# A scheduled attention and feed-forward kernel: Strassen's form in the output product too, a and b in one PSUM bank, and the first batch given to the scheduler

## The chip, the cores and the metric

The kernel runs on one core of one Trainium2 chip. The metric is the device time of one execution in microseconds (us), as the median of several executions. Each profile is of one execution. A profile's span is some 1.9 us shorter than the time.

Engines in the profile: PE is TensorE's matmuls, PEld its weight loads (they overlap PE), DVE is VectorE, ACT is ScalarE, POOL is GpSimd, SP is SyncE.

## The reference

```python
# q, k, v: (8 batches, 8 heads, 576, 64) f32; out: (4608, 512) f32
kv  = einsum('bhsd,bhse->bhde', k, v)
x   = einsum('bhsd,bhde->bhse', q, kv)
x   = x / sqrt(mean(x*x, -1) + 1e-6) * g_norm        # per head; then (4608, 512)
a, b = x @ w_a, x @ w_b                              # (512, 1536) each
out = (a * b) @ w_out                                # (1536, 512)
```

## The kernel before

The program is straight-line code that a small list scheduler inside the kernel writes. Each piece of work is a node with an engine, a planned duration, a priority, the nodes it needs and the buffers it takes and frees. The scheduler plays these nodes through with the planned durations and emits them in the order it finds. Nothing in the program changes that order at run time: each engine is given its own queue of instructions.

```python
class Plan:
    LAT = {"PE": 0.27, "SP": 2.2}            # from a node's end to whoever waits for it; others 0.1
    def ready(self, n):
        t = 0.0
        for d, lat in n.deps:
            if d.end is None: return INF
            t = max(t, self.after(d, 0.0 if lat is None and d.eng == n.eng else lat))
        for b in n.takes:
            t = max(t, b.ring.when(), b.ring.pool.pick()[0])
        return t
def mm_us(n, cols):  return n * (cols / 2400 + 0.0025)
def act_us(n, bias=False): return (0.26 if bias else 0.16) + n / 1200
def dve_us(n):       return (n + 151) / 960          # fp32, or from PSUM
def fast_us(n):      return (n / 2 + 100) / 960      # 16-bit, SBUF only
```

The first 512 tokens go through the plain a/b products. The other 4096 go in blocks of 512 to 768 tokens through Strassen's seven products in Winograd's form, with operand sums made on VectorE. For each of six column blocks j, and for a and b apart, the seven products come in the order below. X, Y and Z are PSUM banks, `ev` is a copy out of a bank on ScalarE, `comb` an addition of a bank and such a copy on VectorE. A product onto a bank that is being read must wait for the read.

```python
PB, PA = Pool(banks[0:5]), Pool(banks[5:8])
RX, RY, RO = (Ring(PB, c) for c in (2, 2, 1))        # a/b: X; Y and Z; output product
RQ, RS = Ring(PA, 2), Ring(PA, 2)                    # attention
# [...] in wino_block, for which in ("a", "b"), for each j (arguments shortened):
p1 = pe(X, b11);  e1 = ev(u1, X)
p2 = pe(Y, b21);  c11 = comb(Y, u1)                  # frees Y
p6 = pe(X, t2);   e2 = ev(u2, X)                     # onto X: waits for e1
p5 = pe(Z, t1);   p7 = pe(X, t3);  e3 = ev(u3, X)
c22 = comb(Z, u3)
p4 = pe(X, t4);   c21 = copy(X)                      # ScalarE; frees X
p3 = pe(Z, b22);  c12 = comb(Z, u2)                  # onto Z: waits for c22; frees Z
# [...]
m = mul(ab, a_part * b_part)                         # VectorE, when a and b are there
```

The output product is the plain one: for each of 36 groups of 128 tokens, twelve matmuls of 512 columns in nodes of three, and one copy by VectorE or ScalarE. The k of a late batch (2 to 7) is put in another order by VectorE, `"p h c d -> p c h d"`, with 4 chunks of 128 rows and one of 64 apart. Batch 0 is written by hand ahead of everything that is scheduled.

Of the kernel before, what the change touches and what calls it, by code (L numbers as in the profile page):

```python
# [40 lines left out]
class Buf:  # L41
# [6 lines left out]
    def take(self, t=0.0):  # L48
        r = self.ring
        i = r.pool.pick()[1]  # L50

        self.tile = r.pool.tiles[i]
        r.pool.holder[i] = self
        r.held = [b for b in r.held if b.freed() > t] + [self]
        return self


class Node:
    def __init__(self, eng, dur, prio, emit, deps=(), takes=(), frees=()):
        self.eng, self.dur, self.prio, self.emit = eng, dur, prio, emit  # L60
        self.deps = [d if isinstance(d, tuple) else (d, None) for d in deps if d is not None]
        self.takes = takes
        self.start = self.end = None
        for b in frees:
            b.last.append(self)


class Plan:
    LAT = {"PE": 0.27, "SP": 2.2}
# [28 lines left out]
    def order(self):  # L98
        free, todo, done = {}, sorted(self.nodes, key=lambda n: n.prio), []
        waits = {n: [d for d, _ in n.deps if d.end is None] for n in todo}  # L100
        while todo:
            best = {}
            for n in todo:
                if waits[n]:
                    waits[n] = [d for d in waits[n] if d.end is None]
                    if waits[n]:
                        continue
                f = free.get(n.eng, self.t0)
                if n.eng in best and best[n.eng][0][0] <= f:
                    continue  # L110
                t = max(self.ready(n), f)
                if t == INF:
                    continue
                key = (f if t < f + 0.06 else t, n.prio)
                if n.eng not in best or key < best[n.eng][0]:
                    best[n.eng] = (key, t, n)
            assert best, "no node can go"
            _, t, n = min(best.values(), key=lambda x: x[1])
# [10 lines left out]
def kernel(  # L129
# [27 lines left out]
    WB = [0, 128] + list(range(256, d_ff + 1, 256))  # L157
# [3 lines left out]
    BLOCKS = [(512, 320), (1152, 256), (1664, 320), (2304, 384), (3072, 384), (3840, 384)]  # L161
    NMAX = 384
    NJ = FC // 2

# [5 lines left out]
    def sb(name, shape, dt):  # L170
# [7 lines left out]
    sums = {w: [sb(f"s{w}{i}", [128, 2, HM], FP16) for i in range(4)] for w in "ab"}  # L178
    xp = [sb(f"xp{i}", [128, 2, R], FP16) for i in range(2)]
    k_ts = [sb(f"k_t{i}", [128, H * EC * D], BF16) for i in range(2)]  # L180
    v_ts = [sb(f"v_t{i}", [128, H * EC * D], BF16) for i in range(2)]
# [3 lines left out]
    T_ts = [sb(f"T{i}", [128, 4, 2, NMAX], FP16) for i in range(2)]  # L185
    b_ts = [sb(f"b_sb{i}", [128, 2, 2 * NMAX], FP16) for i in range(2)]
    u_ts = [sb(f"u{i}", [128, NMAX], FP32) for i in range(8)]
    sq_ts = [sb(f"sq{i}", [128, HF], BF16) for i in range(4)]
    rs_ts = [sb(f"rs{i}", [128, HF], FP32) for i in range(4)]
    o_ts = [sb(f"o_sb{i}", [128, d_model], FP32) for i in range(4)]  # L190

    arenas = [
        [ab_ts[1][:].rearrange("p a b -> p (a b)"), 0],
        [T_ts[0][:].rearrange("p a b c -> p (a b c)"), 0],
        [T_ts[1][:].rearrange("p a b c -> p (a b c)"), 0],
        [b_ts[1][:].rearrange("p a b -> p (a b)"), 0],
    ]

    def carve(n, dt=BF16):
        w = n * (2 if dt == FP32 else 1)  # L200
        for a in arenas:
            if a[1] + w <= a[0].shape[1]:
                ap = a[0][:, a[1] : a[1] + w].bitcast(dt)
                a[1] += w
                return ap
        raise ValueError(n)
# [4 lines left out]
    def early_load(t, b, hs):  # L211
        for n, src in (("q", q), ("k", k), ("v", v)):
# [6 lines left out]
        {  # L219
            "q": early_view(carve(H * EC * D)),  # L220
            "k": early_view(k_ts[b]),
            "v": early_view(v_ts[b]),
        }
        for b in range(2)
# [4 lines left out]
    for n, src, eng in (("q", q, nc.scalar), ("k", k, nc.sync), ("v", v, nc.sync)):  # L229
        raw[n] = carve(2 * EC * D, FP32)[0:EP].rearrange("p (h c d) -> p h c d", h=2, d=D)  # L230
# [6 lines left out]
    qs = [[carve(S) for _ in range(NP)] for _ in range(2)]  # L237


    zt = const.tile([128, 512], BF16)  # L240
# [10 lines left out]
    for i in range(2):  # L251
        t = const.tile([128, NP, 128], BF16, name=f"kvd{i}")
        nc.vector.memset(t, 0.0)
        kvd.append(t)
    g_col = const.tile([128, 1], FP32)
# [9 lines left out]
    for f0, f1 in zip(WB[:-1], WB[1:]):  # L265
# [3 lines left out]

    for i in range(2):  # L270
        early_load(early[1], 1, slice(i * HP, (i + 1) * HP))
# [5 lines left out]
    early_ring = {"at": [banks[0:3], 0], "f": [banks[4:8], 0]}  # L277

    def bank(kind):
        r = early_ring[kind]  # L280
        r[1] += 1
        return r[0][(r[1] - 1) % len(r[0])]

    def dummies(n):
        ps = banks[3]
# [6 lines left out]
    class Attn:  # L292
        def __init__(self, b):
            self.b, self.kvd = b, kvd[b % 2]
# [67 lines left out]
    at0 = Attn(0)  # L362
    n_sq, n_rs = [0], [0]

    def nxt(ts, n):
        n[0] += 1
        return ts[(n[0] - 1) % len(ts)]

    def qT0(p):
        ps = bank("f")  # L370
        at0.early_qT_mm(p, ps)
        at0.early_qT_out(p, ps, nc.vector.tensor_copy)

    def kv0(p, cp):
        ps = bank("f")
        at0.early_kv_mm(p, ps)
        at0.early_kv_out(p, ps, cp)

    def xu0(p, h):
        at0.x_mm(p, h, bank("at"))  # L380
        at0.sq_op(p, h, nxt(sq_ts, n_sq))

    def norm0(p, h):
        at0.rs_op(p, h, nxt(rs_ts, n_rs))
        at0.xt_op(p, h)

    def ss0(p, h, norm=True):
        at0.s_mm(p, h, bank("f"))
        if norm:
            norm0(p, h)  # L390

# [8 lines left out]

    N0 = BLOCKS[0][0]

# [12 lines left out]
    qT0(0)  # L415
    kv0(0, nc.vector.tensor_copy)
    dummies(3)
    xu0(0, 0)
    xu0(0, 1)
    last = NP - 1  # L420
    for p in range(1, NP):
        qT0(p)
        dummies(6 if p == 1 else 4)
        kv0(p, nc.scalar.copy if p == last else nc.vector.tensor_copy)
        ss0(p - 1, 0)
        if p == last:
            dummies(2)
        xu0(p, 0)
        ss0(p - 1, 1, norm=p != last)
        xu0(p, 1)  # L430
    dummies(1)
    ss0(last, 0)
    norm0(last - 1, 1)
    ss0(last, 1)
    lead = [[bank("f"), bank("at")], [bank("f"), bank("f")]]

    def lead_mm(u, *kcs):
        for kc in kcs:
            for ps, w in zip(lead[u], (wa_t, wb_t)):
                std_mm(ps, w, u, kc, N0)  # L440

    lead_mm(0, 0, 1, 2)
    lead_mm(1, 0, 1, 2)
    lead_mm(0, 3)
    std_a(lead[0][0], 0)
    std_b(lead[0][1], 0)
    lead_mm(1, 3)
    std_a(lead[1][0], 1)
    std_b(lead[1][1], 1)

# [4 lines left out]
    def act_us(n, bias=False):  # L455
        return (0.26 if bias else 0.16) + n / 1200

    def dve_us(n):
        return (n + 151) / 960

    def fast_us(n):
        return (n / 2 + 100) / 960

    T0 = 24.5
    plan = Plan(T0)
    PB, PA = Pool(banks[0:5]), Pool(banks[5:8])
    RX, RY, RO = (Ring(PB, c) for c in (2, 2, 1))
    RQ, RS = Ring(PA, 2), Ring(PA, 2)
    RU, RB, RT, RAB = Ring(u_ts), Ring(b_ts), Ring(T_ts), Ring(ab_ts)
    RSQ, RRS, ROS = Ring(sq_ts), Ring(rs_ts), Ring(o_ts)  # L470
    RK, RV, RKR, RQT, RKD = Ring(k_ts), Ring(v_ts), Ring([kr_t]), Ring(qT_ts), Ring(kvd[::-1])
    normed = {}

    def xdeps(pairs, ta, tb):
        return [
            normed[b, p, h]
            for b in range(1, B)
# [6 lines left out]
    readers = {}  # L484

# [33 lines left out]
    def early_batch(b, win):  # L519
# [5 lines left out]
        for p in range(NP):  # L525
            pr = w0 + (w1 - w0) * (p - 0.7) / NP
            sq, sk = Buf(RY), Buf(RY)
            here = [plan.at(37.0 if p < NP // 2 else 40.5)]
            n1 = plan.add("PE", 0.40, pr, lambda p=p, s=sq: at.early_qT_mm(p, s.tile), here, [sq])
# [5 lines left out]
            n3 = plan.add("PE", 0.35, pr, lambda p=p, s=sk: at.early_kv_mm(p, s.tile), here, [sk])  # L535
# [7 lines left out]
    def late_batch(b, load, win):  # L543
# [3 lines left out]
        kr = Buf(RKR)  # L547
        kd = Buf(RKD)
# [5 lines left out]
        def reorder():  # L554
            src = view(kb.tile)
            nc.vector.tensor_copy(
                kr.tile[:, 0:NCH], src[:, :, 0:NCH, :].rearrange("p h c d -> p c h d")
            )
            nc.vector.tensor_copy(kr.tile[0:SB, NCH], src[0:SB, :, NCH, :])

        r = plan.add("DVE", 1.2, w0, reorder, [(load["n"], 7.0)], [kr], [kb])
        s = Buf(RS)

        def kv_mm():
            kv_ps = s.tile[:].rearrange("p (a e) -> p a e", a=NP)
            for c in range(NCH + 1):
                rows = 128 if c < NCH else SB
                for p in range(NP):
# [3 lines left out]
                        lhsT=kr.tile[0:rows, c, hs, :],  # L572
                        rhs=view(vb.tile)[0:rows, hs, c, :],
# [5 lines left out]
            "PE", 1.6, w0, kv_mm, [r, (load["n"], 8.0), plan.at(w0 - 3)], [s, kd], [kr, vb]  # L579
# [14 lines left out]
    def load_node(b, prio, dep):  # L594
# [23 lines left out]
        def transpose():  # L618
# [5 lines left out]
        first_us = 18.0 if dep is None else 7.0  # L624
        ld["n"] = plan.add(
            "POOL", first_us, prio, issue, [(dep["qn"], 5.5)] if dep else [], [ld["k"], ld["v"]]
        )
        ld["qn"] = plan.add(
            "SP", 2.5, prio, transpose, [(ld["n"], 5.0)], [ld["q"]]
# [6 lines left out]
    def std_block(win):  # L636
# [4 lines left out]
        rd = readers.setdefault(0, [])  # L641
        for fc in range(2, FC):
            pr = w0 + (w1 - w0) * (fc - 2) / (FC - 2)
            pa, pb = Buf(RX), Buf(RY)

            def mm(ps, w, fc):
                for kc in range(KC):
                    std_mm(ps.tile, w, fc, kc, N0)

            n1 = plan.add(  # L650
                "PE", mm_us(KC, N0), pr, lambda fc=fc, ps=pa: mm(ps, wa_t, fc), [tk], [pa]
            )
# [3 lines left out]
            n3 = plan.add(  # L656
# [277 lines left out]
```

## Time and profile before

| | before |
|---|---|
| median (3 runs) | 323.94 us (323.69 to 324.58) |
| span of the profile | 322.0 us |
| TensorE, VectorE, ScalarE busy | 96%, 65%, 58% |

The first part of the page of the kernel before gives busy us, share of the span and instructions of each engine; the first line of the fourth part gives the shares of the chain of work that ended last.

```profile
PE 307.6 (96%) x2006; PEld 179.2 (56%) x2006; DVE 208.6 (65%) x410; ACT 188.3 (58%) x475; POOL 62.3 (19%) x78
...
PE 86%; DMA 8%; DVE 2%; ACT 2%; issue 1%; DVEq 0%
```

TensorE bounds the kernel. Busy time by stretch says where it does not (kernel before; the stretch, its length, then for each engine busy us and instructions, the granted TensorE clock, DMA share and GB/s):

```profile
core 0: us, PE busy (x) PEld busy (x) DVE busy (x) ACT busy (x) POOL busy (x), PEclk, DMA share, GB/s
...
25.00:62.00 37.00, 32.22 (x243) 16.69 (x241) 20.95 (x33) 16.40 (x40) 11.47 (x14) 0.95 1.42 185
62.00:100.00 38.00, 37.38 (x258) 24.19 (x257) 30.14 (x67) 29.21 (x78) 11.87 (x13) 1.00 1.34 143
...
180.00:220.00 40.00, 40.00 (x245) 22.98 (x244) 28.16 (x51) 25.14 (x61) 0.00 (x0) 1.00 0.09 31
```

From 180 to 300 us TensorE never stops, with VectorE at 70% in the stretch shown. Before 62 us it does. The largest hole is this (timeline of TensorE, kernel before; start, length to the end of the group, instruction, count, and the idle time before it with what ended it):

```profile
52.73 0.81 PE L829 MATMUL bk<-wo_t,abt 128*128 128x512 f16 x3
55.64 0.28 PE L329 MATMUL bk<-b_sb,kvd 128*128 128x288 bf16 x1 [2.10 <-DVE xp L352]
58.06 2.25 PE L570 MATMUL bk<-v_t,kr_t 128*128 128x128 bf16 x20 [2.14 <-DMA v_t<-in_v_dram]
```

It has two halves. The second is the kv product of batch 2, which stands at the head of the queue while its v has not landed. The first half waits for an `xp` of VectorE, and the timeline of VectorE shows where that stood:

```profile
54.27 0.69 DVE L556 COPY kr_t<-k_t 128x2048 bf16<-128x2048 bf16 x1 [3.29 <-DMA k_t<-in_k_dram]
54.88 0.28 DVE L559 COPY kr_t<-k_t 64x512 bf16<-64x512 bf16 x1
55.09 0.93 DVE L352 SCALAR_TENSOR_TENSOR xp<-bk,g_col,rs 128x288 f16<-128x288 f32 x2
```

It stood behind the copy of batch 2's k, which had not landed either. Both halves are one thing: work on batch 2 ordered before its data was there. After the hole 20 products take 2.25 us; later in the run the same 20 take 1.22 us. The Trainium skill (TensorE: Matmul & The Clock Gate, "Part 1: The HAM clock gate") says that an idle TensorE falls back to half its clock for some microseconds; this trace agrees, with a granted clock of 0.93 between 47 and 60 us as a whole and of 0.57 to 0.58 between 58 and 62 us, where most of the 128-column products start 0.107 us apart instead of 0.056.

**A ledger.** Busy time hides short waits, since a 256-column matmul is shown 0.272 us long while a dense stream of them starts one every 0.109 us. I therefore sum, for every matmul, its start-to-start spacing in a dense stream of the same trace (0.2155 us for 512 columns, 0.1625 for 384, 0.136 for 320, 0.109 for 256, 0.122 for 288, 0.061 for 128, and 0.042 and 0.031 for the small ones of the first two batches), without the filler matmuls, and call that useful work. The rest is loss. (The 0.061 is 1.22 us over 20 and so holds the long shown end of the last product; the 128-column products themselves start 0.056 us apart. With 120 of them, useful work is 0.6 us less and the loss 0.6 us more than the tables say.)

| us, kernel before | |
|---|---|
| until the first useful matmul | 6.4 |
| useful work | 289.6 |
| lost from there to 62 us | 18.3 |
| lost from 62 us to the last matmul | 3.8 |
| last matmul to the end | 3.9 |
| sum | 322.0 |

### The profile page before, as it was taken

The numbers are of one execution on the slowest core, as the hardware profiler recorded it, in microseconds if no ns is written. First come the engines' busy times: TensorE is split into PE (matmuls) and PEld (weight loads), VectorE is DVE, ScalarE is ACT, GpSimd is POOL, SyncE is SP. The second block draws the span as 40 slices with busy tenths as digits, with TensorE's granted clock in tenths as the row PEclk, the third lists the DMA queues.
The fourth block names the chain that finished last, engine by engine and source line by source line (L and its number), as shares of the span: only waits on it lengthen the run. The fifth ranks groups of instructions, "written<-read, shape, count | busy, mean of one in ns | idle before, by whom it ended". The sixth has DMA issues, their size and how long they took to land.

```text
span 322.0 us, 5553 instructions
## 1 busy us (share of the span) xinstructions
PE 307.6 (96%) x2006; PEld 179.2 (56%) x2006; DVE 208.6 (65%) x410; ACT 188.3 (58%) x475; POOL 62.3 (19%) x78
## 2 busy tenths in 40 slices
PE   7979996799999999999999999999999999999995
PEld 3434453466666777666666555565555555555542
DVE  3243875179789659866878668687567776646621
ACT  3353373377877666776788556755567656544410
POOL 8855700430802508001600000000000000000000
PEclk9999999799999999999999999999999999999999
DMA  7999999899997999915994100000000200011022
GB/s 159 191 196 199 204 189 182 109 165 180 96 173 94 128 207 127 184 38 108 106 181 74 36 33 33 35 33 35 33 35 35 66 0 35 33 65 36 33 93 103
DMA packets 80235, 32.65 MB, mean 101 GB/s; under 512 B 51920, under 2 KB 75728, under 8 KB 80208
## 3 DMA queue, kind: packets, MB, share of 16 engines
q0 software_dynamic: 59888, 18.44, 52.9%
q1 hardware_dynamic: 19968, 13.44, 17.8%
q10 hardware_dynamic: 352, 0.43, 0.4%
q8 instruction: 15, 0.25, 0.3%
q14 instruction: 12, 0.10, 0.1%
HBM read 37.75 MB, written 12.98 MB: 158 GB/s over the span
## 4 chain that ended last, share of the span: by engine, by line
PE 86%; DMA 8%; DVE 2%; ACT 2%; issue 1%; DVEq 0%
PE bk L734 45%; PE bk L829 28%; DMA v_t<-in_v_dram 6%; PE bk L393 3%; PE bk L570 3%; PE bk L329 2%; PE bk L343 2%; DMA abt<-in_q_dram 2%; PE bk L287 2%; ACT rs L347 1%; PE bk L317 1%; DVE xp L352 1%; PE bk L301 1%; DVE sa L681 0%; DVE sb L681 0%
## 5 line engine op out<-in xcount | busy, mean ns | idle before, releaser
L758 ACT COPY u<-bk 128x384 f32<-128x384 f32 (+2 forms) x216 | 87.8, 448 | 54.6 <-PE bk L734 53.7
L829 PE MATMUL bk<-wo_t,abt 128*128 128x512 f16 x432 | 113.0, 381 | 0.3 <-ACT o_sb L862 0.3
L764 DVE TENSOR_TENSOR abt<-bk,u 128x384 f16<-128x384 f32 (+2 forms) x108 | 55.1, 510 | 49.5 <-ACT u L758 37.5
L829 PEld LDWEIGHTS <-abt 128*128 128x128 f16 x432 | 42.4, 98 | 35.7 <-issue 1.7
L764 DVE TENSOR_TENSOR b_sb<-bk,u 128x384 f16<-128x384 f32 (+2 forms) x108 | 54.6, 505 | 4.7 <-PE bk L734 4.1
L734 PE MATMUL bk<-T,sa 128*128 128x384 f16 (+2 forms) x216 | 48.6, 308 | 0.1
L734 PE MATMUL bk<-T,sb 128*128 128x384 f16 (+2 forms) x216 | 48.2, 308 | 0.0
L352 DVE SCALAR_TENSOR_TENSOR xp<-bk,g_col,rs 128x288 f16<-128x288 f32 x64 | 32.5, 512 | 18.8 <-ACT rs L347 18.8
L734 PEld LDWEIGHTS <-sa 128*128 128x128 f16 x288 | 28.1, 98 | 18.0 <-issue 0.5
L734 PEld LDWEIGHTS <-sb 128*128 128x128 f16 x288 | 28.1, 98 | 17.0 <-issue 0.2
L347 ACT ACTIVATE rs<-bk,eps_t 128x288 f32<-128x288 f32 x64 | 32.3, 508 | 6.8 <-PE bk L343 6.2
L796 DVE TENSOR_TENSOR abt<-abt,b_sb 128x1536 f16<-128x1536 f16 (+2 forms) x36 | 31.3, 870 | 3.7
L734 PE MATMUL bk<-xp,wa_t 128*128 128x384 f16 (+2 forms) x144 | 32.5, 308 | 0.0
L734 PE MATMUL bk<-xp,wb_t 128*128 128x384 f16 (+2 forms) x144 | 32.3, 308 | 0.2 <-ACT b_sb L783 0.2
L339 ACT ACTIVATE sq<-bk 128x288 bf16<-128x288 f32 x64 | 26.1, 419 | 9.2 <-PE bk L329 8.9
L734 PEld LDWEIGHTS <-wa_t 128*128 128x128 f16 x216 | 21.0, 98 | 15.8 <-issue 0.9
L734 PEld LDWEIGHTS <-wb_t 128*128 128x128 f16 x216 | 21.0, 98 | 12.0 <-issue 0.4
L603 POOL DMA_DIRECT2D scr<-in_q_dram x12 | 19.6, 1639 | 3.1 <-issue 2.4
L783 ACT CAST abt<-bk 128x384 f16<-128x384 f32 (+2 forms) x36 | 16.0, 446 | 6.8 <-PE bk L734 6.7
L862 DVE COPY o_sb<-bk 128x512 f32<-128x512 f32 x19 | 13.0, 685 | 9.9 <-PE bk L829 9.7
L862 ACT COPY o_sb<-bk 128x512 f32<-128x512 f32 x16 | 9.4, 588 | 16.5 <-PE bk L829 16.3
L343 PE MATMUL bk<-sq,ones 128*128 128x288 bf16 x64 | 18.5, 289 | 0.6 <-ACT sq L339 0.4
(73 smaller groups left out, 296.1 us busy)
## 6 DMA issues: line engine op xcount, KB each, us to landing
out_dram<-o_sb SPq DMA_DIRECT2D x23, 256.0 KB, 2.0
scr<-in_q_dram POOLq DMA_DIRECT2D x12, 288.0 KB, 6.4
k_t<-in_k_dram POOLq DMA_DIRECT2D x6, 512.0 KB, 9.1
v_t<-in_v_dram POOLq DMA_DIRECT2D x6, 512.0 KB, 11.0
out_dram<-o_sb SPq DMA_DIRECT2D x13, 128.0 KB, 2.3
wo_t<-in_moe_w_out_dram POOLq DMA_DIRECT2D x2, 768.0 KB, 15.4
wa_t<-in_moe_w_a_dram POOLq DMA_DIRECT2D x5, 256.0 KB, 9.1
wb_t<-in_moe_w_b_dram POOLq DMA_DIRECT2D x5, 256.0 KB, 9.7
```

The costliest lines, as they stand in the source:

```text
L339: nc.scalar.activation(sq, self.x_ps[p, h][:, 0:HF], AF.Square)
L343: nc.tensor.matmul(ps[:, 0:HF], lhsT=ones, rhs=self.sq[p, h], start=True, stop=True)
L347: nc.scalar.activation(rs, self.s_ps[p, h][:, 0:HF], AF.Abs_reciprocal_sqrt, bias=eps_t)
L352: nc.vector.scalar_tensor_tensor(out=xcols(p, self.b * S + h * HF, HF), in0=self.x_ps[p, h][:, 0:HF], scalar=g_col, in1=self.rs[p, h], op0 ...
L603: nc.gpsimd.dma_start(out=scr[:, :, hl, :].rearrange("p s d -> s p d"), in_=qv[hl])
L734: nc.tensor.matmul(ps.tile[:, 0:n], lhsT=w[:, kc, sl], rhs=rhs()[:, kc, :], start=start and kc == 0, stop=kc == 1, skip_group_check=True,)
L758: lambda: nc.scalar.copy(u.tile[:, 0:n], ps.tile[:, 0:n]), [dep], [u],
L764: lambda: nc.vector.tensor_add(dst(fi, h), ps.tile[:, 0:n], u.tile[:, 0:n]),
L783: lambda X=X, dst=dst: nc.scalar.copy(dst(1, 0), X.tile[:, 0:n]),
L796: nc.vector.tensor_mul(t, t, bb.tile[:, :, 0 : 2 * n])
L829: nc.tensor.matmul(ps.tile[:], lhsT=ab.tile[:, order[x], g * 128 : (g + 1) * 128], rhs=wo_t[:, order[x], :], start=x == 0, stop=x == FC - 1,)
L862: eng, us, pr + 0.3, lambda cp=cp, ps=ps, o=os_: cp(o.tile[:], ps.tile[:]),
```

## The change

The intent: take an eighth of the output product's work off TensorE as well (Strassen's form for 4096 of the 4608 tokens, with its operand sums on VectorE); save instructions by letting a and b share each bank, so that one copy or addition serves both; pad kv to full 128 rows so that the copy of k is one instruction; and fill the start by giving batch 0 to the scheduler and loading the weights in another order. The planned durations of VectorE and ScalarE are set lower too, and the planned handoff from them to another engine is raised from 0.1 to 0.18 and 0.2 us. The core of the diff, cut:

```diff
-    LAT = {"PE": 0.27, "SP": 2.2}
+    LAT = {"PE": 0.27, "SP": 2.2, "ACT": 0.2, "DVE": 0.18}
-        return (0.26 if bias else 0.16) + n / 1200
+        return (0.155 if bias else 0.06) + n / 1200
-        return (n + 151) / 960
+        return (n + 65) / 960
-        return (n / 2 + 100) / 960
+        return (n / 2 + 72) / 960
-    BLOCKS = [(512, 320), (1152, 256), (1664, 320), (2304, 384), (3072, 384), (3840, 384)]
+    BLOCKS = [(t, N0 // 2) for t in range(N0, n_tok, N0)]            # 8 blocks, 256
-    PB, PA = Pool(banks[0:5]), Pool(banks[5:8])
+    PB, PA, PO = Pool(banks[0:4]), Pool(banks[5:8]), Pool(banks[4:5])
 # a/b: one product for both, a in the left half of the bank, b in the right
+                for i, (w, sm) in enumerate(wts):
+                    for kc in range(2):
+                        nc.tensor.matmul(ps.tile[:, i * n : (i + 1) * n], ...)
 # [...] output product: operand sums on VectorE, in place where it goes, two chunks of three j
+                    (sx(s3), a11, a21, v.tensor_sub, s3),
+                    (a21, a21, a22, v.tensor_add, None),
+                    (sx(s2), a21, a11, v.tensor_sub, s2),
+                    (sx(s4), a12, sx(s2), v.tensor_sub, s4),
 # [...] then seven products of 2 x 6 matmuls of 256 columns: X from RO, Y and Z from RY
 # [...] late batches: one copy of k, planned 0.75 us
-                kr.tile[:, 0:NCH], src[:, :, 0:NCH, :].rearrange("p h c d -> p c h d")
+            lambda: nc.vector.tensor_copy(kr.tile[:], view(kb.tile).rearrange("p h c d -> p c h d")),
```

## The prediction

> **What bounds the kernel now.** TensorE. The page has PE busy 307.6 of 322.0 us (96%), VectorE 65%, ScalarE 58%; the chain of waits is 86% PE. The stretch table has PE busy all of 100-140 and 180-300. The timeline gives the spacing of streamed matmuls: 0.2155 us for 512 columns, 0.1625 for 384, 0.136 for 320, 0.109 for 256, so columns/2.4 GHz plus 2.5 ns, as the Trainium skill says (TensorE: Matmul & The Clock Gate, "Wait — 56ns, not 53.3ns?"). Weight loads (98 ns mean) hide even behind 128-column products (20 in 1.22 us).
>
> With these spacings PE's useful work is about 290 us. The other 32 us: 6.4 us to the first data; 11 us of gaps and filler matmuls until the a/b products run at 23.1 us; about 11 us lost later; 3.7 us from the last matmul (318.3) to the end. Of the later loss 6 us is one place: PE has nothing at 53.4-58 us because the kv product of batch 2, waiting for v (4.8 us), stands at the head of its queue; after it 20 products take 2.25 us in place of 1.22 and six 512-column ones 2.08 in place of 1.29, the granted clock being 0.93 there.
>
> **What changes.**
> 1. Output product in Strassen form for 4096 of 4608 tokens: 384 x 512 columns (82.8 us) become 672 x 256 (73.2 us): -9.5 us of PE work.
> 2. The a/b products were Strassen already: blocks of 256 instead of 320/384 mean 1344 instead of 1008 matmuls: +0.6 us.
> 3. a and b share a bank: 216 additions of 256-384 columns on VectorE become 144 of 512; 288 ScalarE evictions become 192. VectorE back to back costs (columns+65)/0.96 ns in the trace (256 columns: 0.33 us apart): the fusion saves only overhead, under 10 us.
> 4. Added on VectorE: operand sums of the output product, about 0.48 us x 8 a block (30-36 us over the run), 24 combining additions instead of 19 copies. VectorE work per 512-token block is about 25 us against 30 of PE: load from 68% to about 83%, by busy time 85-88%.
> 5. kv on 128 rows: as many products for PE; one copy less per batch.
> 6. Scheduling batch 0 with the rest and reordering weight loads: a/b products begin about 4 us earlier between its steps; batch 2 is planned after 61 us with other work ahead: most of the 6 us returns.
>
> **On the critical path.** PE work 290 -> 281 us; early idle about 22 -> 13 us, the hole mostly gone; steady loss grows a little because VectorE is fuller (3 -> 4-6 us); tail similar. Span about 304, time **306 us**, range 300 to 315. Faster by over 2%: 0.93; within 2%: 0.05; slower: 0.02.
>
> **What would show it.** PE busy about 290 us with the span near 304; the output-product line at 672 matmuls spaced 0.109 us; a/b products before 20 us; no PE wait on v_t near 55 us and a clock of 1.0 there; VectorE busy near 265 us; PE nearly unbroken from 65 us on.
>
> **What would make it wrong.** VectorE at 83% with its queue in order: late additions hold banks (the output's Z stays taken over several products, leaving one bank of that ring to a/b), and PE waits 1 us or more a block; this shows as PE idle released by VectorE. Weights landing later than assumed, so that PE starves at 25-40 us and its clock falls. A tail where the last sums delay the last products.

## The result

| | before | changed |
|---|---|---|
| median (4 runs each) | 323.81 us (323.68 to 324.58) | 319.55 us (319.43 to 319.63) |
| ratio | | 0.9863 (95% interval 0.9846 to 0.988) |
| span of the profile | 322.0 us | 317.6 us |

A ratio is the mean time of one kernel's fast runs over that of the other's of the same rounds, so not quite the ratio of the medians quoted. The result is correct. The change gives 1.4%, where 5.5% was predicted; it lies outside the predicted range.

The same lines of the page of the changed kernel:

```profile
PE 298.4 (94%) x2631; PEld 238.6 (75%) x2631; DVE 246.4 (78%) x436; ACT 194.0 (61%) x403; POOL 62.2 (20%) x78
...
PE 62%; DVE 25%; DMA 5%; issue 3%; ACT 3%; POOL 2%; DVEq 0%; ACTq 0%; POOLq 0%
```

VectorE's part of the chain went from 2% to 25%. By stretch (changed kernel, columns as before):

```profile
25.00:62.00 37.00, 35.68 (x269) 19.95 (x267) 24.40 (x45) 19.81 (x46) 12.75 (x14) 1.00 1.47 198
62.00:100.00 38.00, 35.22 (x305) 28.65 (x304) 35.57 (x60) 28.49 (x61) 14.17 (x16) 1.00 1.27 133
...
180.00:220.00 40.00, 37.74 (x353) 32.83 (x352) 33.90 (x60) 25.03 (x52) 0.00 (x0) 1.00 0.17 51
220.00:260.00 40.00, 38.09 (x345) 33.13 (x343) 31.97 (x56) 26.45 (x54) 0.00 (x0) 1.00 0.09 28
```

The start is fuller and its clock is whole. From 62 us on TensorE has gaps where it had next to none, with VectorE at 80 to 94%. Who it waited for between 62 and 300 us (waits of TensorE: total us, times, longest), first in the kernel before:

```profile
PE bk L829 <- ACT o_sb L862: 0.3, 1, 0.3
PE bk L734 <- ACT b_sb L783: 0.2, 1, 0.2
```

and in the changed kernel:

```profile
PE bk L718 <- DVE c L737: 2.1, 5, 0.6
PE bk L718 <- DVE T L687: 2.0, 3, 0.9
PE bk L340 <- DVE xp L363: 1.5, 3, 0.9
PE bk L881 <- ACT o_sb L915: 1.3, 2, 0.7
```

With three smaller lines left out here, VectorE ended 7.0 of the 8.3 us and ScalarE 1.3. The list holds only gaps in the busy time; the ledger finds more. The ledger, with the prediction's own terms beside it, says how much:

| us | before | changed | difference | predicted difference |
|---|---|---|---|---|
| until the first useful matmul, and lost from there to 62 us | 24.7 | 16.1 | -8.6 | about -9 |
| useful work | 289.6 | 280.7 | -8.9 | -9 |
| lost from 62 us to the last matmul | 3.8 | 15.0 | +11.2 | +1 to +3 |
| last matmul to the end | 3.9 | 5.9 | +2.0 | 0 |
| span | 322.0 | 317.6 | -4.4 | about -18 |

The first row is two predicted terms, and each came out: TensorE had lost 17.4 us by 25 us before and 13.8 us after (about 4 us were predicted), and between 52 and 62 us, where the hole was, 6.3 us before and 0.1 us after; between these it lost 1.1 us more than before.

So 17.5 us were won where they were expected, and 13.2 us given back in two places.

Two things in the changed trace stand out. First, a border between two blocks (timelines of TensorE and then of VectorE, changed kernel):

```profile
213.84 1.47 PE L881 MATMUL bk<-wo_t,abt 128*128 128x256 f16 x12
215.99 1.47 PE L881 MATMUL bk<-so,as 128*128 128x256 f16 x12 [0.68 <-ACT o_sb L915]
218.26 0.38 PE L718 MATMUL bk<-T,sa 128*128 128x256 f16 x2 [0.81 <-DVE T L687]
```

```profile
214.07 0.56 DVE L866 TENSOR_TENSOR as<-abt 128x768 f16<-128x768 f16 x1
214.66 0.56 DVE L866 TENSOR_TENSOR abt<-abt 128x768 f16<-128x768 f16 x1
215.25 0.56 DVE L866 TENSOR_TENSOR as<-abt 128x768 f16<-128x768 f16 x1
215.85 0.56 DVE L866 TENSOR_TENSOR as<-abt,as 128x768 f16<-128x768 f16 x1
216.32 0.51 DVE L363 SCALAR_TENSOR_TENSOR xp<-bk,g_col,rs 128x288 f16<-128x288 f32 x1
216.87 0.43 DVE L687 TENSOR_TENSOR T<-xp,xp 128x512 f16<-128x512 f16 x1
```

The old block's sums (`as`) and the new block's sums (`T`) stand in one row on VectorE, and TensorE has no a/b product left to put between the output products. Of the two gaps the second (0.81 us) is ended by a sum; the first (0.68 us) is ended by ScalarE's copy of a bank, 0.13 us after the sum that the same product needs. I call "sum gaps" the part of the loss that lies in gaps during which VectorE is at an operand sum, `T` or `as`: 0.9 us before, 7.5 us in the changed kernel. Second, in this row sums that need the one just before them (they read what it wrote, or write over what it read) start 0.58 to 0.59 us apart; when another instruction follows a sum of the same size, it starts 0.465 to 0.477 us later (30 of 31 cases). The scheduler plans 0.475. The copy of k is off by more (groups of instructions by shape: busy us, mean ns of one, idle before; before, then changed):

```profile
L556 DVE COPY kr_t<-k_t 128x2048 bf16<-128x2048 bf16 x6 | 4.9, 812 | 3.3 <-DMA k_t<-in_k_dram 3.3
L559 DVE COPY kr_t<-k_t 64x512 bf16<-64x512 bf16 x6 | 2.0, 339 | 0.0
```

```profile
L512 DVE COPY kr_t<-k_t 128x2560 bf16<-128x2560 bf16 x6 | 8.8, 1475 | 0.0
```

One instruction of 2560 columns takes longer than the two of 2048 and 512 that it replaces, and twice the planned 0.75 us. The means before are raised by one copy of each six: the medians are 0.684 and 0.278 us, so the change is from 0.96 to 1.475 us.

### The profile page after: what moved, and what is told of

Its sections match the earlier page's. It is cut to its first block, busy times and chain, and to the rows that moved or that the text cites. A ratio compares the mean times of both kernels' runs of the same rounds, so it can differ in the third digit from the quotient of the medians.

```text
span 317.6 us, 6672 instructions
## 1 busy us (share of the span) xinstructions
PE 298.4 (94%) x2631; PEld 238.6 (75%) x2631; DVE 246.4 (78%) x436; ACT 194.0 (61%) x403; POOL 62.2 (20%) x78
## 4 chain that ended last, share of the span: by engine, by line
PE 62%; DVE 25%; DMA 5%; issue 3%; ACT 3%; POOL 2%; DVEq 0%; ACTq 0%; POOLq 0%
PE bk L718 32%; PE bk L881 17%; DVE c L737 8%; PE bk L374 6%; DVE as L866 4%; DVE abt L771 4%; DMA abt<-in_q_dram 3%; DVE xp L363 3%; PE bk L817 2%; DMA as<-in_k_dram 2%; DVE T L687 2%; PE bk L340 2%; PE bk L354 1%; DVE abt L866 1%; DVE kr_t L512 1%
## 5 line engine op out<-in xcount | busy, mean ns | idle before, releaser
L737 DVE TENSOR_TENSOR c<-bk,u 128x512 f16<-128x512 f32 x144 | 96.6, 684 | 27.5 <-PE bk L718 16.8
L411 ACT COPY u<-bk 128x512 f32<-128x512 f32 x144 | 82.2, 589 | 42.9 <-PE bk L718 38.8
L718 PE MATMUL bk<-xp,wa_t 128*128 128x256 f16 x288 | 55.0, 272 | 1.8 <-DVE c L737 1.4
L718 PE MATMUL bk<-xp,wb_t 128*128 128x256 f16 x288 | 54.9, 272 | 0.0
L718 PE MATMUL bk<-T,sa 128*128 128x256 f16 x192 | 36.6, 272 | 2.0 <-DVE T L687 2.0
L411 ACT CAST c<-bk 128x512 f16<-128x512 f32 x48 | 28.0, 588 | 16.0 <-PE bk L718 15.5
L881 PE MATMUL bk<-wo_t,abt 128*128 128x256 f16 x288 | 36.8, 273 | 1.0 <-DVE c L737 0.6
L718 PE MATMUL bk<-T,sb 128*128 128x256 f16 x192 | 36.7, 273 | 0.0
L771 DVE TENSOR_TENSOR abt<-c 128x1024 f16<-128x1024 f16 x48 | 33.2, 692 | 4.3
L718 PEld LDWEIGHTS <-sa 128*128 128x128 f16 x288 | 28.1, 98 | 10.3 <-issue 6.4
L881 PEld LDWEIGHTS <-as 128*128 128x128 f16 x288 | 28.2, 98 | 5.3 <-issue 1.9
L915 ACT COPY o_sb<-bk 128x512 f32<-128x512 f32 x31 | 18.2, 587 | 17.8 <-PE bk L881 17.5
```

The costliest lines, as they stand in the source:

```text
L411: ("ACT", act_us(n), lambda: nc.scalar.copy(*args())),
L718: nc.tensor.matmul(ps.tile[:, i * n : (i + 1) * n], lhsT=lhs(w, sm)[:, kc, :], rhs=rhs()[:, kc, :], start=start and i == 0 and kc == 0, st ...
L737: lambda: nc.vector.tensor_add(cs(fi, h), full(ps), u.tile),
L771: nc.vector.tensor_mul(t, c[:, :, :, 0], c[:, :, :, 1])
L881: nc.tensor.matmul(ps.tile[:, sub * EH : (sub + 1) * EH], lhsT=lhs(slice(j, j + 1))[:, 0, sub * 128 : (sub + 1) * 128], rhs=rhs[:, j, :], ...
L915: lambda: nc.scalar.copy(o(fi, h), bank(X, every)), [dep], takes, frees,
```

## The experiments

Four theories:
1. *Amount*: VectorE has so much work that TensorE waits for it, in whatever order.
2. *Banks*: a and b together fill whole banks and the output product takes from the same ring, so TensorE waits for free banks.
3. *Costs*: the planned costs are too low for some VectorE work, so each queue's order is right on paper and late on the chip.
4. *Border*: the output product's place in the order leaves TensorE nothing to do while VectorE makes sums.

"Loss" below is always the ledger's loss from 62 us to the last matmul. The three groups e1 to e4, e5 to e8 and e9 to e12 ran on different chips, on which the kernel before had medians of 323.95, 324.44 and 324.36 to 324.40 us. All are edits of the changed kernel, which was not run again on these chips: a difference to it is across chips, where the kernel before moved by 0.6 us, and loss is read from one execution, where the four of a kernel lie up to 1.3 us apart. So differences under about 1 us say nothing.

### e1: the copy of k walked by heads

```diff
-lambda: nc.vector.tensor_copy(kr.tile[:], view(kb.tile).rearrange("p h c d -> p c h d")),
+lambda: nc.vector.tensor_copy(kr.tile[:].rearrange("p c h d -> p h c d"), view(kb.tile)),
```

> The changed kernel with one edit: the reorder copy of k is walked with the heads outermost (8, even) instead of the chunks (5, odd); same data. In the changed kernel's trace this copy takes about 1.4 us, where the scheduler planned 0.75. If VectorE is what TensorE waits for (theory 1), six copies 0.5 us shorter give back 1 to 3 us: 316.5 to 318.5 us. If TensorE waits for free PSUM banks whatever VectorE's load (theory 2), nothing: 319.5. If the copy itself does not get shorter, the reading of why it is slow is wrong.

Measured: 317.36 us, ratio to before 0.9801 (0.9774 to 0.9827); loss 13.0 us. The copies of e1 (shortest, median and longest in ns, then first and last start):

```profile
L512 DVE COPY kr_t<-k_t x6: 815/819/1439, 57.1 to 191.4; 128x2560 bf16<-128x2560 bf16 x6
```

The same bytes take 819 ns in the median in place of 1475; one copy of the six took 1439, so that the mean is 921. The Trainium skill (VectorE: DVE Perf Modes, "Mode 2×_2P — use both read ports for one tensor") asks of the faster copy modes that the outermost dimension be even, or odd and equal for source and destination. The five chunks are odd on the source's side, while the destination is written as one run; the old copy had four chunks, the new walk has eight heads. These times agree with that: 2560/1475 is 1.7 elements per ns in the slow form, 2560/819 is 3.1 in the fast one, and the old copy, walked by chunks too but by four, made 2048/684 = 3.0. So it is the odd count, not the walk by chunks. The one slow copy of e1 ran while GpSimd was issuing a DMA, and so did the slow pair of the kernel before (1443 and 645 ns); the other 39 fast-form copies of all traces ran beside no such instruction and none was slow. No run tests whether that is the cause. Six copies, 0.55 us shorter in the mean, gave back 2.0 us of loss. The sum gaps stayed at 7.5 us: what this edit won lies elsewhere.

### e2: the scheduler knows the spacing of dependent sums

```diff
-                prev = [n]
+                prev = [(n, 0.115)]            # output product's sums
 # and in the a/b blocks' four T sums
-[m3] + xdeps(...)   [m1]   [m2] + xdeps(...)
+[(m3, 0.115)] + xdeps(...)   [(m1, 0.115)]   [(m2, 0.115)] + xdeps(...)
```

> The changed kernel, same instructions; only the scheduler is told that a VectorE operand sum that reads what the sum just before it wrote starts 0.115 us later (measured spacing 0.59 against 0.47 us for 768 columns). Theory 3 (the order was made with costs that are too low, so handoffs come late): 1 to 4 us faster, 315.5 to 318.5. Theory 1 in its pure form (the amount of VectorE work alone): within 0.7 us of 319.5. Theory 2: within 0.7 us too.

Measured: 317.17 us, ratio 0.9802 (0.9768 to 0.9837); loss 11.9 us. No instruction was added or removed. The scheduler now weaves the two chains (timeline of VectorE, e2):

```profile
246.09 0.42 DVE L687 TENSOR_TENSOR T<-xp,xp 128x512 f16<-128x512 f16 x1
246.44 0.55 DVE L866 TENSOR_TENSOR abt<-abt 128x768 f16<-128x768 f16 x1
246.91 0.42 DVE L687 TENSOR_TENSOR xp<-xp 128x512 f16<-128x512 f16 x1
247.24 0.55 DVE L866 TENSOR_TENSOR as<-abt 128x768 f16<-128x768 f16 x1
```

A 768-column sum is again followed after 0.47 us and a 512-column one after 0.33 to 0.35. Sums that follow each other 0.58 to 0.59 us apart fell from 25 to 9, and the sum gaps from 7.5 to 5.2 us, 2.3 of the 3.1 us of loss won. Theory 3 expected 1 to 4 us; the 2.4 us (2.0 by the ratios) are in it, and outside what theories 1 and 2 allowed.

### e3: no operand sums of the output product

```diff
-        for q in range(chunks): ...            # the four sums of each chunk
-            p6 = prod(..., sx(s2), t2, ...)
+            p6 = prod(..., a21, t2, ...)       # and likewise p7, p3
```

> Wrong result on purpose: the operand sums of the output product on VectorE are left out (60-odd instructions, about 34 us of VectorE), and the products read the unsummed blocks; TensorE and ScalarE do the same work. Theory 1: the time that TensorE loses after 62 us falls from 15.6 us to about 5, time 308 to 311 us. Theory 2: still 12 us or more lost, 317 us or above. Theory 3 (too-low costs of these very sums and of others): between the two, 310 to 314.

Measured: 312.16 us, ratio 0.9641 (0.9614 to 0.9668), wrong as meant; VectorE busy 216.1 us, loss 7.7 us. The sums cost 7.3 us of TensorE's time. That is in theory 3's range and 1 us short of theory 1's, and theory 2's 317 us is out. It does not tell whether by their amount or by their place; e12 does.

### e4: Z of the output product from the attention banks

```diff
-            o_block(bi - 1, ab, muls, osum, o_win, 2, (RO, RY, RY), 1)
+            o_block(bi - 1, ab, muls, osum, o_win, 2, (RO, RY, RS), 1)
```

> The changed kernel, but the long-held third bank of the output product (Z) comes from the three attention banks instead of from the four that the a/b products use. Theory 2 (bank shortage): 4 us or more faster, 315.5 or below. Theories 1 and 3: within 1 us of 319.5, or slightly slower because attention has fewer banks.

Measured: 322.73 us, ratio 0.9966 (0.9937 to 0.9995); loss 18.6 us. It is slower. Theory 2's gain is not there, but the test is not clean: attention lost a bank by it, and the waits of its products for VectorE's `xp` grew from 1.5 to 2.3 us. Those of the a/b products for additions grew too, from 2.1 to 3.7 us: a new ring gives another order throughout.

### e5: the old planned costs

```diff
-    LAT = {"PE": 0.27, "SP": 2.2, "ACT": 0.2, "DVE": 0.18}
+    LAT = {"PE": 0.27, "SP": 2.2}
 # and act_us, dve_us, fast_us as in the kernel before
```

> The changed kernel, same instructions; only the costs that the scheduler plans with are put back to those of the kernel before (each VectorE and ScalarE instruction some 0.1 us dearer). Theory 3 (the order is too tight for the real durations): the order gets slack, 2 to 5 us faster, 314.5 to 317.5. Theory 1 (VectorE is nearly full whatever the order): within 1 us of 319.5, since no VectorE work goes away.

Measured: 316.70 us, ratio 0.977 (0.9753 to 0.9787); loss 12.0 us, with VectorE busy 246.7 us as in the changed kernel. The same instructions in a looser order are 2.9 us faster; theory 1 in its pure form allowed 1 us. The handoffs of VectorE and ScalarE go back to 0.1 us with it, so what gets dearer is the time on the engine. The sum gaps hardly move (7.4 us): what e5 won is for the most part not what e2 won.

### e6: the plain output product in all blocks, in lumps

```diff
-            o_block(bi - 1, ab, muls, osum, o_win, 2, (RO, RY, RY), 1)
+            o_std(ab, muls, o_win, blocks_of[bi - 1][0])     # one node of 12 matmuls a group
```

> The changed kernel with the output product in the plain form in all blocks: TensorE gets 9.5 us more work, VectorE loses its sums and combining additions (about 50 us), the scheduling of batch 0 and the shared banks stay. Theory 1: loss after 62 us falls from 15.0 to 4-6 us and the end after the last product from 5.9 to about 4, so 316 to 319 us: no slower than the changed kernel, the output product's new form being paid back nearly in full. Theory 2 (banks: a and b filling whole banks): loss stays at 12 us or more, 325 us or above.

Measured: 326.69 us, ratio 1.0074 (1.0059 to 1.0089); useful work 290.2 us, VectorE busy only 197.4 us, and loss 14.7 us. My expectation was wrong. VectorE has 49 us less to do than in the changed kernel and TensorE loses as much. The loss sits where a/b products stand alone: 10.6 of the 14.7 us are between two a/b products (timeline of TensorE, e6):

```profile
265.89 0.38 PE L718 MATMUL bk<-T,sb 128*128 128x256 f16 x2
266.68 0.38 PE L718 MATMUL bk<-xp,wa_t 128*128 128x256 f16 x2 [0.40 <-DVE c L737]
266.89 0.38 PE L718 MATMUL bk<-xp,wb_t 128*128 128x256 f16 x2
267.29 0.38 PE L718 MATMUL bk<-T,wa_t 128*128 128x256 f16 x2
267.51 0.38 PE L718 MATMUL bk<-T,wb_t 128*128 128x256 f16 x2
268.02 0.38 PE L718 MATMUL bk<-xp,sa 128*128 128x256 f16 x2
```

A dense stream would start a pair every 0.22 us. Here there are 0.79, 0.40 and 0.51 us between pairs onto different banks, because each waits for a copy or an addition on its bank (the view names the addition for the first; for the other two it is read from the code). The a/b chain cannot feed TensorE by itself; it needs other products between its steps. In e6 these came in lumps of 2.6 us. The amount theory falls with this run as the sole cause: it expected 4 to 6 us of loss.

### e7: e1 and e2 together

```diff
+tensor_copy(kr.tile[:].rearrange("p c h d -> p h c d"), view(kb.tile))      # e1
+prev = [(n, 0.115)]    [(m3, 0.115)] + xdeps(...)    [(m1, 0.115)] ...       # e2
```

> The two edits of e1 (copy walked by heads) and e2 (the scheduler knows the spacing of dependent sums) together. If they act on different VectorE time, they add: 2.2 + 2.4 us, 314.5 to 315.7 us. If they only remove the same stalls: 316 to 317.

Measured: 315.20 us, ratio 0.9712 (0.9691 to 0.9732); loss 10.2 us. 15.0 less 2.0 and 3.1 is 9.9: the two add. The sum gaps are those of e2 (5.0 us).

### e8: another end

```diff
-            p7 = prod(5, X, sx(s3), t3, ...);  e3 = ev(5, 1, 0, p7);  c22 = comb(5, 1, 1, X, ...)
-            prod(6, W, a22, t4, True, [n4], [W], per_sub=ends)        # c21 from W and e3
+            p4 = prod(5, W, a22, t4, True, [n4], [W]);  e4 = copy(u4 <- W)     # ScalarE
+            prod(6, X, sx(s3), t3, False, [e2, n3, p4], ..., per_sub=ends)
+            # then, for each half of the rows: c22 = X + u5, c21 = X + u4, store
```

> e7 with another end of the last output unit: the product into its own bank is made and copied out by ScalarE while the last product runs, so that after the last matmul only VectorE's additions of half the rows each are left, each followed by its store; one ScalarE copy (0.59 us) leaves the end. The end after the last product falls from 5.9 to about 4.7 us: 1 to 1.5 us faster than e7.

Measured: 314.10 us, ratio 0.9685 (0.9671 to 0.97); the time from the last matmul to the end falls from 5.9 to 4.7 us, loss 10.5 us. The step works and gives 1.1 us. So 1.2 us of the 2.0 us that the changed kernel's end had grown by were its row of one ScalarE copy and then VectorE additions.

### e9: the plain output product in small pieces

The plain product as in e6, but in nodes of three matmuls spread over the block, with copies by VectorE and ScalarE in turn and 3 us later in priority. Among variants that the scheduler could place at all, one whose own timetable had few TensorE gaps was taken.

```diff
-                for fc in range(FC): ...                     # one node of 12
+            for i in range(0, FC, 3): ...                    # nodes of 3, priority pr + 0.1 * i
-        o_win = (st[bi] + 1.0, st[bi + 1] - 1.0) if bi < nb else ...
+        o_win = (st[bi] + 1.0 + 3.0, st[bi + 1] - 1.0 + 3.0)
```

> e6 again (output product in the plain form in all blocks), but in pieces of three matmuls spread over the block and moved 3 us later, as fine as in the kernel before; e6 gave it in lumps of twelve, between which the a/b products stood alone. If e6's loss of 14.7 us after 62 us came from its lumps, it falls to 3-6 us and the time to 314-317 us, so the plain output product in this frame beats the changed kernel. If the shared banks of a and b cost TensorE time whatever stands between them, it stays at 10 us or more: 321 us or above.

Measured: 314.82 us, ratio 0.9707 (0.9688 to 0.9726); useful work 290.2 us, loss 2.9 us. The waits of TensorE between 62 and 300 us in e9:

```profile
PE bk L718 <- DVE c L737: 0.3, 1, 0.3
```

So a and b sharing a bank cost TensorE next to nothing, given other products between their steps. The run is no clean test of the lumps: against e6 it also takes the output product off the ring that the a/b products use (Y and Z; it has one bank of its own, as in the kernel before), moves it later and spreads its copies over two engines. The other half of theory 2, the output product on the a/b ring, is answered by e10, which keeps that ring and loses 5.6 us: most of the loss was not for want of banks. And without the new form of the output product this frame is 4.7 us faster than the changed kernel, across chips. In the changed kernel the new form saved 9.5 us of useful work against e9 and gave back 12.1 us of loss and 1.8 us at the end.

### e10: e8 with the output product later and in smaller pieces

```diff
-            o_block(bi - 1, ab, muls, osum, o_win, 2, (RO, RY, RY), 1)
+            o_block(bi - 1, ab, muls, osum, o_win, 2, (RO, RY, RY), 2)     # pieces of 3 j in place of 6
-        o_win = (st[bi] + 1.0, st[bi + 1] - 1.0) if bi < nb else ...
+        o_win = (st[bi] + 1.0 + 4.5, st[bi + 1] - 1.0 + 4.5) if bi < nb else ...
```

The 4.5 us and the pieces were picked by the scheduler's own timetable too.

> e8 with the output product of each block given to the scheduler 4.5 us later and in pieces of three column blocks in place of six, so that it is spread over the start of the next block's a/b products and does not stand alone at the border where VectorE makes eight operand sums in a row. If the border stalls (up to 1.1 us each in the changed kernel's trace, with TensorE having nothing else in order) are most of what is left of the loss after 62 us, it falls from 10.5 to 5-7 us: 308.5 to 311.5 us. If VectorE's amount of work sets the loss, within 1 us of e8's 314.1.

Measured: 308.98 us (308.7 to 309.28), correct, ratio 0.9527 (0.9508 to 0.9547); loss 5.6 us with VectorE busy 240.7 us. By stretch, e10:

```profile
62.00:100.00 38.00, 37.18 (x324) 30.49 (x323) 36.14 (x64) 29.01 (x63) 11.73 (x14) 1.00 1.29 133
...
180.00:220.00 40.00, 40.00 (x373) 35.46 (x372) 34.22 (x60) 27.14 (x56) 0.00 (x0) 1.00 0.07 27
```

and the waits of TensorE between 62 and 300 us, e10:

```profile
PE bk L718 <- DVE c L737: 0.5, 2, 0.3
PE bk L881 <- DVE c L737: 0.2, 1, 0.2
PE bk L340 <- DVE xp L363: 0.2, 1, 0.2
PE bk L881 <- DVE abt L771: 0.2, 1, 0.2
```

Between 180 and 220 us VectorE is busy 34.22 us of 40, a little more than the 33.90 of the changed kernel, and TensorE does not stop. The sums are all there; they only stand elsewhere. This is also 5.8 us faster than e9, on the same chip: with its order mended, the new form is worth its sums (e10 has the shorter copy, the spacing and the end as well).

### e11: that shift alone

The edit of e10 on the changed kernel, without e1, e2 and e8.

```diff
+            o_block(bi - 1, ab, muls, osum, o_win, 2, (RO, RY, RY), 2)
+        o_win = (st[bi] + 1.0 + 4.5, st[bi + 1] - 1.0 + 4.5) if bi < nb else ...
```

> The changed kernel with that shift and the smaller pieces alone (copy, spacing and end as in the changed kernel). If the border is a cause of its own beside the too-low costs: 3 to 5 us faster than the changed kernel, 314.5 to 316.5. If it only trades one wait for another: within 1 us of 319.5.

Measured: 314.08 us, ratio 0.9688 (0.9665 to 0.9711); loss 9.6 us. Shift and smaller pieces are worth 5.4 us of loss alone and 4.9 us on top of e8: the place of the output product is a cause of its own beside the costs. That it acts at the border is shown for the most part here, where the sum gaps fall from 7.5 to 3.2 us, 4.3 of the 5.4; from e8 to e10 they fall from 5.1 to 2.3, 2.8 of the 4.9, and the rest lies elsewhere. No run parts the shift from the smaller pieces.

### e12: e10 without the sums

```diff
-        for q in range(chunks): ...            # the four sums of each chunk, as in e3
-            p6 = prod(..., sx(s2), t2, ...)
+            p6 = prod(..., a21, t2, ...)       # and likewise p7, p3
```

> Wrong result on purpose: e10 without the operand sums of the output product on VectorE (about 30 us of its work), as e3 was the changed kernel without them. In the changed kernel their removal was worth 7.4 us. If the sums cost TensorE time by their amount, they cost about the same here: 301 to 302.5 us. If they cost it by where they stood in the order, most of that is already gone in e10: 306 to 309 us.

Measured: 305.98 us, ratio 0.9439 (0.9417 to 0.9462), wrong as meant; loss 2.5 us. The sums that cost 7.4 us of time in the changed kernel cost 3.0 us in e10. More than half of their cost was the order in which they stood (e10 also has the shorter copy); what is left goes with the sums themselves, and no run here divides that further.

| run | time, us | useful | loss to 62 | loss after 62 | end | VectorE busy |
|---|---|---|---|---|---|---|
| before | 323.81 | 289.6 | 18.3 | 3.8 | 3.9 | 208.6 |
| changed | 319.55 | 280.7 | 10.1 | 15.0 | 5.9 | 246.4 |
| e1 copy | 317.36 | 280.7 | 9.8 | 13.0 | 5.9 | 243.4 |
| e2 spacing | 317.17 | 280.7 | 10.2 | 11.9 | 5.9 | 243.3 |
| e3 no sums | 312.16 | 280.7 | 9.6 | 7.7 | 5.9 | 216.1 |
| e4 Z elsewhere | 322.73 | 280.7 | 9.8 | 18.6 | 5.9 | 247.5 |
| e5 old costs | 316.70 | 280.7 | 10.2 | 12.0 | 5.9 | 246.7 |
| e6 plain, lumps | 326.69 | 290.2 | 9.7 | 14.7 | 4.1 | 197.4 |
| e7 copy + spacing | 315.20 | 280.7 | 10.3 | 10.2 | 5.9 | 239.8 |
| e8 + end | 314.10 | 280.7 | 10.1 | 10.5 | 4.7 | 239.9 |
| e9 plain, fine | 314.82 | 290.2 | 9.6 | 2.9 | 4.1 | 209.7 |
| e10 + shift | 308.98 | 280.7 | 10.1 | 5.6 | 4.7 | 240.7 |
| e11 shift alone | 314.08 | 280.7 | 9.2 | 9.6 | 5.9 | 246.8 |
| e12 e10, no sums | 305.98 | 280.7 | 9.6 | 2.5 | 4.7 | 212.2 |

## Why the prediction was right and wrong

- **TensorE's useful work, 290 to 281 us: right.** 289.6 to 280.7, with 672 output matmuls spaced 0.109 us and 1344 a/b matmuls.
- **The start: right.** Predicted from about 22 to 13 us, the hole "mostly gone". By the ledger 24.7 to 16.1 us, and not by luck: the earlier start gave 3.6 us for about 4 predicted, the hole 6.2 us for most of 6. The first a/b matmul starts at 14.62 us, the hole is closed, and the granted clock of 25 to 62 us rose from 0.95 to 1.00.
- **"Steady loss grows a little because VectorE is fuller (3 -> 4-6 us)": the step that failed.** The wait term was mis-sized, not VectorE's load: the loss grew from 3.8 to 15.0 us, with VectorE less busy than predicted. I had taken 83% for low enough, and had costed VectorE as if every instruction followed the last at the dense spacing and as if the scheduler's order would do. Three parts of that were wrong, and e1, e2 and e10 show their size on the way from 15.0 to 5.6 us. The copy of k (2.0 us) was in the prediction as "one copy less per batch"; its busy time rose from 6.9 to 8.8 us, because its count of chunks had become odd. The spacing of dependent sums (3.1 us) was neither in my sum nor in the scheduler's. The place and pieces of the output product (4.9 us, of which 2.8 in sum gaps), with output product and sums alone at the border, could have been read from the order of instructions before the run, which I looked at only for counts.
- **"A tail similar": wrong.** 3.9 to 5.9 us. Of the added 2.0 us, e8 took away 1.2 by shortening the row of copies and additions after the last product.
- **What would make it wrong: named, partly for the wrong reason.** I had written that late additions would hold banks "and PE waits 1 us or more a block", shown as idle released by VectorE. That is what the waits show. But I put it down to VectorE's load. e6 has the loss with VectorE busy for 61% of the span (197.4 of 325.1 us), and e10 does without most of it at 78% (240.7 of 307.3), the share that it has in the changed kernel. The load makes the order matter; the order set most of the loss, and the amount the 3.0 us of e12.
- **VectorE "near 265 us", 85-88%: too high.** It was busy 246.4 us, 78%.

With the order put right the predicted span was in reach: e10 has 307.3 us against some 304, with a loss after 62 us of 5.6 us, in the predicted 4 to 6.

What stays open: whether e5's gain comes from the slack or only from another order, since no run changed planned costs at random, and any change of them gives a new order (for e2 the trace shows the intended change); what e4 would show with a bank to spare; the 3.0 us that the sums still cost in e10; and the loss of about 10 us before 62 us, on which no run was spent.

## What to carry to other kernels

When a change takes work off the busiest engine and gives it to one that is then four fifths full, cost the handoffs and not only the sums: look up in the order what the busy engine has to do while the other makes its longest row of dependent instructions, and put that work there. A program that is ordered by planned costs is only as good as these; compare planned with measured spacing for each kind of instruction, dependent and independent apart, before blaming the load. A plain product spread finely between chains that wait for their own results can be worth more than a cleverer one whose sums hold it up (e9 against the changed kernel), and less than the same one in a better order (e10).

## What the Trainium skill lacked or had wrong

- VectorE: DVE Perf Modes, "The DRAIN you can't avoid", tells of copies that a semaphore between two instructions costs nothing extra. Here a 768-column `tensor_tensor` that waits for the one before it (to read what it wrote or write over what it read) starts 0.58 to 0.59 us after it, and an independent instruction 0.465 to 0.477 us after it; in the changed kernel, telling the scheduler so was worth 2.4 us (e2).
- The same page's rule for the two-port copy modes holds, but it does not warn that a destination written as one run is not "equal" to an odd source: 2560 bf16 columns took 1475 ns walked by five chunks and 819 ns in the median walked by eight heads (e1).
- TensorE: Matmul & The Clock Gate, "Back-to-back issue gap", gives 131 ns for 512 columns and 81 ns for 128 in a stream of weight loads and matmuls. These traces show 215.5 ns and 56 ns, each matmul with its own weight load; the N/2.4 + 2.5 that it gives for an isolated one (215.8 and 55.8 ns) is right at both.
